# Where a decayed key product, a gate weight, a gather and a weight conversion stand in a fused linear-attention and MoE kernel

## The chip, the cores and the metric

The kernel runs on one core of a Trainium2 chip. The metric is the device time in microseconds (us) of one execution. In the text PE is TensorE, DVE is VectorE, ACT is ScalarE, GpSimd is the engine that the profile calls POOL, and SP is SyncE, which issues most of the DMAs. Each engine runs its own instructions in its own order and waits for the others through semaphores.

## What is computed

A linear attention with a decay for every channel, whose output is the input of a mixture of eight experts with one expert for each token, followed by a dense MLP with a squared relu:

```python
state = alpha[:, :, t, :, None] * state + np.einsum('bhd,bhe->bhde', k[:, :, t], v[:, :, t])
y[:, :, t] = np.einsum('bhd,bhde->bhe', q[:, :, t], state)
...
logits = x @ w_gate + modality_bias[modality_id]
e_idx = np.argmax(logits, axis=1)
...
gate_w = probs[np.arange(N), e_idx]
h = np.maximum(x[mask] @ w1[e], 0.0)
out[mask] = gate_w[mask, None] * (h @ w2[e])
...
h = x @ w_in
r = np.maximum(h, 0.0)
return (r * r @ w_out).astype(np.float32)
```

There are 4 sequences of 768 tokens with 8 heads of 48 channels, so 3072 tokens of 384 values. An expert has a hidden width of 1024, the last MLP one of 2048.

## The kernel before

**Attention.** The 3072 tokens are 24 chunks of 128, six to a sequence. `prep(n)` makes, on DVE, the running product of the decay (`acum`, a scan, L455), its reciprocal (L457), a scan in the other direction (`rs`, L459, the decay from a token to the chunk's end), the scaled queries `qt` (L461) and the scaled keys `kt` (L463). `kt` has three buffers, `rs` one. A chunk is prepared three chunks ahead of its use. `qk_mm` multiplies keys and queries on PE (`sp`, L476), ACT copies the result out (`pa`, L479), and GpSimd cuts away the future tokens (`pm`, L481, two instructions for a chunk). `k_T` transposes `kt` on PE. `kv_mm` makes the chunk's addition to the state on PE (`kv`, L502 and L506), and DVE scales the state (`sd`, L509). ACT copies it into block form (`sbd`, L516 and L517), and `y_mm` (L526, L531) makes the output `y`, which ACT copies (`yt`, L533).

**Gating.** It follows the chunks in groups of 8, 8, 5 and 3. For a group: the logits on PE (`lg`), the one-hot choice on DVE (`gate_a`, into `oh_all`), the exponentials on ACT (`gate_e`, `ex`), matmuls on PE that count each token's rank within its expert (`gate_b`, `rk`), arithmetic of seven DVE instructions on that rank (`gate_c`, L249 to L258), and the gate's weight (`gate_s`, L270 to L273: a sum, an addition and a reciprocal, `gw`). `scale(t)` then transposes a chunk's output on PE (`xtr`, L281), and two ACT instructions scale it by `gw` (`xb`, L285); SP stores it. PE writes `xtr` into a PSUM buffer that `xb` has to have read before the next `xtr`.

**Experts.** The tokens of the experts go through eight slots. Slots 0 and 1 hold 2 blocks of 128 tokens, slots 2 to 6 hold 4, slot 7 is small. `gather(i)` has GpSimd issue one indirect DMA for each block (L607), into `xg`, which has one buffer. `x_T1` transposes the gathered tokens on PE (`xt`, L625). `s1` and `s2` are the two layers, each product made of three matmuls (L632 to L634) on a high and a low half of the operands. Weights are loaded as `raw` and split into halves by ACT (L542) and DVE (L543, `w1l`, `w2l`); `pop()` does one waiting split or load.

**Conversion.** Beside the slots, the last MLP's weights, which arrive as 64-bit numbers, are converted to fp32 in 24 steps. A step is a load (`conv_load`), five DVE instructions (L694 to L698) and one ACT instruction (`conv_v`), two GpSimd products of 128x512 (`conv_g`, L705 and L706) and a store (`conv_store`). `conv_tick((2, 0, 1))` stores one block, loads another and computes a third. The tile `cvt` in which a step ends has two buffers, and the same two hold `r`, the hidden layer of the last MLP.

**The last MLP** works on six chunks of 512 tokens with 16 steps `f` each: `m1` (relu on ACT, L984; square on DVE, L985; a split) and `m2`, into `acc`. Indirect DMAs write the rows out.

**What sets the order.** It is written out by hand. The attention loop has named places in each chunk, "pre", "kv", "pool", "mid" and "end", and `at(n, place, fn)` puts work into them; `do(n, place)` runs what is there. In the loop, `qk_mm(n + 1)` comes ahead of `prep(n + 3)`, that ahead of "mid", then `y_mm(n)` and "end". In the slots the order is that of the loop over `f`, with `conv_tick` at the listed values of `f`.

Of the kernel before, what the change touches and what calls it, by code (L numbers as in the profile page):

```python
# [18 lines left out]
ALU = mybir.AluOpType  # L19
# [37 lines left out]
def body(ctx, tc, qka, v, alpha, mod, wg, mbias, w1, w2, w_in, w_out, out):  # L57
    nc = tc.nc
    V, A, G, PE, SY = nc.vector, nc.scalar, nc.gpsimd, nc.tensor, nc.sync
# [174 lines left out]
    def gate_b(g):  # L234
        t0, T = GROUPS[g]
        ohb = oh_all[:, t0:t0 + T + 1, :]
        rk = ps_g.tile([128, GM + 1, NE], F32, tag="rk", name="rk")[:, :T + 1, :]
        PE.matmul(rk, lt_b, ohb, start=True, stop=False)
        for i in range(T):
            PE.matmul(rk[:, i + 1:, :], ones_b, ohb[:, i:i + 1, :].to_broadcast([128, T - i, NE]), start=False, stop=(i == T - 1))  # L240
        gst[g]["rk"] = rk

    def gate_c(g):
        t0, T = GROUPS[g]
        sh = [128, T, NE]
        rk = gst[g]["rk"]
        oh = oh_all[:, t0:t0 + T, :]
        R = gt.tile(sh, F32, tag="R", name="R")
        V.tensor_tensor(R, rk[:, :T, :], over(run, sh), op=ALU.add)  # L249
        V.tensor_add(run, run, rk[:, T, :])  # L250
        V.tensor_mul(R, R, oh)
        ri = rk_all[:, t0:t0 + T, :]
        V.tensor_reduce(ri, R, axis=AX.X, op=ALU.max)
        V.tensor_scalar(rhx_all[:, t0:t0 + T, :], ri, 7, 3, op0=ALU.logical_shift_right, op1=ALU.bitwise_xor)
        lo = gt.tile([128, T, 1], I32, tag="lo", name="lo")
        V.tensor_single_scalar(lo, ri, 127, op=ALU.bitwise_and)
        lof = gt.tile([128, T, 1], F32, tag="lof", name="lof")
        V.tensor_copy(lof, lo)  # L258
        gst[g]["lof"] = lof
# [6 lines left out]
    def gate_s(g):  # L266
        t0, T = GROUPS[g]
        ex = gst[g]["ex"]
        ss = gt.tile([128, T], F32, tag="ss", name="ss")
        V.tensor_reduce(ss, ex, axis=AX.X, op=ALU.add)  # L270
        V.tensor_scalar_add(ss, ss, 1e-9)
        gw = gt.tile([128, T], F32, tag="gw", name="gw")
        V.reciprocal(gw, ss)  # L273
        gst[g]["gw"] = gw
# [175 lines left out]
    def prep(n):  # L450
        qk = loaded.pop(n)
        qq, kk = (qk[:, i * NP * C:(i + 1) * NP * C].rearrange("p (a c) -> p a c", c=C) for i in range(2))
        al = qk[:, 2 * NP * C:]
        acum = at2.tile([RP, NP, CA], F32, tag="acum", name="acum", bufs=3)
        V.tensor_tensor_scan(acum.rearrange("p a c -> p (a c)"), al, one0.rearrange("p a c -> p (a c)"), 0.0, op0=ALU.mult, op1=ALU.max)  # L455
        rz = raz[n % NR]
        V.reciprocal(rz[:, :, C + 1], acum[:, :, C])  # L457
        rs = at2.tile([RP, NP, CA], F32, tag="rs", name="rs", bufs=1)
        V.tensor_tensor_scan(rs.rearrange("p a c -> p (a c)")[:, ::-1], al[:, ::-1], rz.rearrange("p a c -> p (a c)")[:, ::-1], 0.0, op0=ALU.mult, op1=ALU.add)  # L459
        qt = xp.tile([RP, NP, C], F32, tag="xl", name="qt", bufs=4)  # L460
        V.tensor_mul(qt, qq, acum[:, :, 1:C + 1])  # L461
        kt = at2.tile([RP, NP, C], F32, tag="kt", name="kt", bufs=3)
        V.tensor_tensor(kt, kk, rs[:, :, 2:], op=ALU.mult)  # L463
        ae = acum[:, :, C:C + 1]
        return dict(ae=ae, qt=qt, kt=kt)

# [265 lines left out]
    def at(n, where, f):  # L732
        todo.setdefault((n, where), []).append(f)
# [16 lines left out]
    for n in range(N):  # L750
        if n + 4 < N:
            loaded[n + 4] = load(n + 4)
        if n + 3 < N:
            vs[n + 3] = load_v(n + 3)
        do(n, "pre")
        kv_mm(n)
        do(n, "kv")
        ts()
        if n + 1 < N:
            qk_mm(n + 1)  # L760
            k_T(n + 1)
        do(n, "pool")
        ts()
        if n + 3 < N:
            preps[n + 3] = prep(n + 3)
        do(n, "mid")
        if n > GROUPS[EG + 1][0] + 3:
            pop(2)
        if n == N - 1:
            x_T(0, 0)  # L770
            x_T(0, 1)
        y_mm(n)
        if n + 1 < N:
            s_bd(n + 1)
        ts()
        if n > 0:
            g, i = tile_group[n - 1]
            t0, T = GROUPS[g]
            if i % 4 == 3 or i == T - 1:
                at(n + 1, "kv", gate_lg(g, i // 4 * 4, i + 1))  # L780
            if i == T - 1:
                late = g > EG
                at(n + 1, "kv", lambda g=g: (gate_a(g), gate_e(g)))
                at(n + 1, "mid" if late else "end", lambda g=g: gate_b(g))
                at(n + 1 if late else n + 2, "end" if late else "kv", lambda g=g: (gate_c(g), gate_s(g)))
                if g == EG:
                    at(n + 2, "mid", early_plan)
                    at(n + 3, "pre", lambda: push(wload(0)))
                    at(n + 4, "mid", lambda: early.append(first_ids(EARLY, 2, ids_e)))
                    at(n + 5, "pool", lambda: (early.pop()(), gather(0)))  # L790
                d = GM if g == EG else 3 if late else 2
                for k in range(T):
                    at(n + (1 if late else 2) + k // 3, "end", lambda t=t0 + k: gate_bt(t))
                    at(n + 2 + k // d, "pre" if late else "pool", lambda t=t0 + k: todo_ts.append(t))
        do(n, "end")
# [95 lines left out]
    mm2(1, 2)  # L891
    x_T1(2, 2)
    mm2_out(1, offset(1), 2, 1)
    conv_tick((2, 0, 1))
    pop()

    soff, sac, shh = {}, {}, {}
# [27 lines left out]
    for i in range(2, NSLOT):  # L925
        last = i == NSLOT - 1
        for f in range(8):
            if f == 0:
                if i > 2:
                    s2(i - 1, 6)  # L930
                drain(("w1", i - 1))
                soff[i] = offset(i)
                perm(i, soff[i])
                if last:
                    push(load_w1(WS, lambda k: wi32[k * 128:(k + 1) * 128, 0:1024]))
                else:
                    gather(i + 1)
                    push(wload(i))
            s1(i, f)
            if f > 0:  # L940
                pop()
            if f in ((0,) if last else (2, 4, 5) if i == 2 else (0, 2, 3, 5)):
                conv_tick((2, 0, 1))
            if last and f == 2:
                push(load_w2(WS, lambda k: wo32[k * 256:(k + 1) * 256, :].rearrange("(f p) d -> p f d", p=128)))
            if f == 5:
                if last:
                    xx2[0] = xsplit(chunks[0], range(1))
                else:
                    x_T1(i + 1, 0)  # L950
            if f == 7:
                if last:
                    xx2[0] = xsplit(chunks[0], range(1, KD), xx2[0])
                else:
                    x_T1(i + 1, 1)
            if f == 1 and i > 2:
                s2(i - 1, 7)
            if f >= 2:
                s2(i, f - 2)
            if f == 7 and not last:  # L960
                x_T1(i + 1, 2)
# [80 lines left out]
    for s in range(len(steps) + LAG):  # L1042
        if s < len(steps):
            ci, f = steps[s]
            if ci > 0:
                i, j = divmod(s - 16, 4)
                if i < NALPHA:
                    if j == 0:
                        alr[i] = alpha_load(i)
                    if j > 1:  # L1050
                        alpha_range(i, j - 2, alr[i])
                elif i == NALPHA and j == 0:
                    fl = rare_flag()
                elif i == NALPHA and j == 2:
                    rare_sum(fl)
            if ci == 0:
                if f in (0, 2, 4):
                    conv_tick((2, 0, 1))
                pop()
                if f == 4:  # L1060
                    w2b()
                if f == 7:
                    drain(("w1", WS + 1))
            more = ci + 1 < len(chunks)
            if f == 13 and more:
                xx2[ci + 1] = xsplit(chunks[ci + 1], range(1))
            m1(s)
        if s >= LAG:
            ci, f = steps[s - LAG]
            if ci == 0 and f == 0:  # L1070
                drain(("w2", WS))
            if ci == 0 and f == 8:
                drain(("w2", WS + 1))
            if s - LAG < len(steps) - TAIL:
                m2(s - LAG)
# [182 lines left out]
```

## Time and profile before

| | us |
| --- | --- |
| time, median of 3 runs | 805.73 (804.85 to 806.98) |
| the profiled execution: its own time | 804.95 |
| the profiled execution: its span | 803.1 |
| PE busy in it | 764.7 |
| DVE busy | 487.1 |
| ACT busy | 336.6 |
| GpSimd busy | 185.4 |

The span runs from the first to the last instruction of the profiled execution, and the busy times are shares of it. An average over the whole kernel says little here: up to about 140 us there is attention, with DVE nearly always busy; from about 150 to 390 us there are the slots, where PE is nearly always busy and GpSimd converts; from about 394 us on there is the last MLP, almost nothing but PE. So each stage is read by itself.

### The profile page before, as it was taken

The numbers are of one execution on the slowest core, as the hardware profiler recorded it, in microseconds if no ns is written. First come the engines' busy times: TensorE is split into PE (matmuls) and PEld (weight loads), VectorE is DVE, ScalarE is ACT, GpSimd is POOL, SyncE is SP. The second block draws the span as 40 slices with busy tenths as digits, with TensorE's granted clock in tenths as the row PEclk, the third lists the DMA queues.
The fourth block names the chain that finished last, engine by engine and source line by source line (L and its number), as shares of the span: only waits on it lengthen the run. The fifth ranks groups of instructions, "written<-read, shape, count | busy, mean of one in ns | idle before, by whom it ended". The sixth has DMA issues, their size and how long they took to land.

```text
span 803.1 us, 12832 instructions
## 1 busy us (share of the span) xinstructions
PE 764.7 (95%) x5007; PEld 672.5 (84%) x5007; DVE 487.1 (61%) x811; ACT 336.6 (42%) x622; POOL 185.4 (23%) x177
## 2 busy tenths in 40 slices
PE   6998988799899999999899999999999999999995
PEld 5787867799688888889789999999999999999985
DVE  7999998468589678697773444544544343343340
ACT  2556667425344534445553332332243233333240
POOL 6344434023464444342110010010000002002001
PEclk8999999899999999999999999999999999999998
DMA  8775876157777588778530030022000001000001
GB/s 220 186 212 153 231 192 218 58 143 218 232 162 272 201 164 262 157 231 185 145 120 0 1 118 27 1 82 63 1 11 31 0 1 40 1 1 30 11 1 43
DMA packets 42557, 88.78 MB, mean 111 GB/s; under 512 B 11149, under 2 KB 26535, under 8 KB 42487
## 3 DMA queue, kind: packets, MB, share of 16 engines
q1 hardware_dynamic: 39287, 78.04, 35.1%
q0 software_dynamic: 3200, 9.83, 3.7%
q8 instruction: 41, 0.67, 0.4%
q14 instruction: 29, 0.24, 0.1%
HBM read 72.10 MB, written 15.76 MB: 109 GB/s over the span
## 4 chain that ended last, share of the span: by engine, by line
PE 75%; DVE 3%; DMA 3%; ACT 2%; issue 2%; POOL 0%; SPq 0%; POOLq 0%; ACTq 0%; DVEq 0%
PE acc L634 8%; PE acc L632 8%; PE acc L633 8%; PE h L633 8%; PE h L634 8%; PE h L632 8%; PE oo L632 4%; PE hps L632 4%; PE oo L634 4%; PE oo L633 4%; PE hps L633 4%; PE hps L634 4%; DMA xg<-xs,ids 1%; PE xt L625 1%; DMA wo<-cvt 1%
## 5 line engine op out<-in xcount | busy, mean ns | idle before, releaser
L985 DVE TENSOR_TENSOR r<-r 128x512 f32<-128x512 f32 x96 | 67.7, 705 | 147.4 <-ACT r L984 147.3
L632 PE MATMUL acc<-w2h,hh 128*128 128x384 f32 x372 | 125.4, 337 | 3.0 <-ACT hh L542 3.0
L634 PE MATMUL acc<-w2h,hl 128*128 128x384 f32 x372 | 125.7, 338 | 0.3 <-DVE hl L543 0.2
L633 PE MATMUL acc<-w2l,hh 128*128 128x384 f32 x372 | 124.9, 336 | 0.0
L984 ACT ACTIVATE r<-h 128x512 f32<-128x512 f32 x96 | 57.4, 598 | 159.5 <-PE h L634 153.9
L634 PE MATMUL h<-xh,w1l 128*128 128x512 f32 x288 | 113.8, 395 | 0.0
L633 PE MATMUL h<-xl,w1h 128*128 128x512 f32 x288 | 113.6, 395 | 0.0
L632 PE MATMUL h<-xh,w1h 128*128 128x512 f32 x288 | 112.1, 389 | 0.0
L1008 POOL DMA_INDIRECT out_dram<-ob,pidx x24 | 23.9, 997 | 366.2 <-ACT ob L1006 326.8
L543 DVE TENSOR_TENSOR hl<-r,hh 128x512 fp32r<-128x512 f32 x93 | 64.5, 694 | 63.8 <-PE acc L634 37.1
L542 ACT CAST hh<-r 128x512 fp32r<-128x512 f32 x93 | 57.7, 620 | 78.7 <-DVE r L985 78.7
L632 PEld LDWEIGHTS acc<-w2h,hh 128*128 128x128 f32 x372 | 69.9, 188 | 7.8 <-ACT hh L542 3.8
L633 PEld LDWEIGHTS acc<-w2l,hh 128*128 128x128 f32 x372 | 69.8, 188 | 3.8
L634 PEld LDWEIGHTS acc<-w2h,hl 128*128 128x128 f32 x372 | 69.8, 188 | 0.9 <-DVE hl L543 0.9
L632 PE MATMUL oo<-hh,w2h 128*128 128x512 f32 (+1 forms) x192 | 69.3, 361 | 0.0
L632 PE MATMUL hps<-xh,w1h 128*128 128x512 f32 (+1 forms) x192 | 68.0, 354 | 1.2 <-ACT xb L285 0.7
L481 POOL TENSOR_SCALAR_AFFINE_SELECT pm<-pa 128x512 f32<-128x512 f32 x48 | 52.1, 1108 | 73.0 <-ACT pa L479 72.9
L634 PE MATMUL oo<-hh,w2l 128*128 128x512 f32 (+1 forms) x192 | 67.7, 353 | 0.0
L633 PE MATMUL oo<-hl,w2h 128*128 128x512 f32 (+1 forms) x192 | 67.6, 352 | 0.0
L633 PE MATMUL hps<-xl,w1h 128*128 128x512 f32 (+1 forms) x192 | 67.1, 350 | 0.0
L634 PE MATMUL hps<-xh,w1l 128*128 128x512 f32 (+1 forms) x192 | 67.1, 349 | 0.0
L634 PEld LDWEIGHTS h<-xh,w1l 128*128 128x128 f32 x288 | 54.0, 187 | 11.5
(220 smaller groups left out, 1360.2 us busy)
## 6 DMA issues: line engine op xcount, KB each, us to landing
qk<-qka_dram SPq DMA_DIRECT2D x23, 675.5 KB, 5.3
raw<-w_dram SPq DMA_DIRECT2D x21, 512.0 KB, 5.7
raw<-w_dram SPq DMA_DIRECT2D x28, 384.0 KB, 3.5
cvr<-w_in_dram SPq DMA_DIRECT2D x12, 512.0 KB, 7.0
cvr<-w_out_dram SPq DMA_DIRECT2D x12, 512.0 KB, 11.1
vv<-v_dram SPq DMA_DIRECT2D x24, 192.0 KB, 6.3
xs<-xb SPq DMA_DIRECT2D x24, 192.0 KB, 3.1
alr<-alpha_dram SPq DMA_DIRECT2D x9, 512.0 KB, 3.7
```

The lines of the kernel that those rows point to most:

```text
L481: G.affine_select(out=pmt, in_=pa, pattern=[[0, 4], [1, C]], compare_op=ALU.is_ge, fill=0.0, base=0, channel_multiplier=-1)
L542: A.copy(hi, raw)
L543: V.tensor_sub(lo, raw, hi)
L625: PE.transpose(xt[:, hf * 128:(hf + 1) * 128], xgs[i][:, hf, k * 128:(k + 1) * 128], ident)
L632: PE.matmul(o, ah, bh, start=start, stop=False)
L633: PE.matmul(o, ah, bl, start=False, stop=False)
L634: PE.matmul(o, al, bh, start=False, stop=stop)
L984: A.activation(r, o, AF.Relu)
L985: V.tensor_mul(r, r, r)
L1008: G.indirect_dma_start(out=out, out_offset=bass.IndirectOffsetOnAxis(ap=pidx[:, n:n + 1], axis=0), in_=ob, in_offset=None)
```

## The change

It has four parts.

1. The product `kt` (L463) is made by GpSimd, not by DVE. The operands and the buffers are the same.
2. The gate's weight `gate_s` moves. For the first two groups it stood with `gate_c` in the "kv" place two chunks on; now it stands at the "end" of the chunk before, right behind the rank matmuls. For the last two groups it moves from "end" to "mid" of the same chunk.
3. The conversion's steps move: the one ahead of slot 2 is gone, slot 2 has four (it had three), slots 3 to 6 have five each (they had four), slot 7 and the last MLP's first chunk have none (they had one and three). All 24 are done by slot 6.
4. The second half of the `w_out` load of the last MLP (`w2b`) is put in the list at step 1 of the first chunk, not at step 4.

```diff
@@ prep
         kt = at2.tile([RP, NP, C], F32, tag="kt", name="kt", bufs=3)
-        V.tensor_tensor(kt, kk, rs[:, :, 2:], op=ALU.mult)
+        G.tensor_tensor(kt, kk, rs[:, :, 2:], op=ALU.mult)
@@ attention loop
-                at(n + 1, "mid" if late else "end", lambda g=g: gate_b(g))
-                at(n + 1 if late else n + 2, "end" if late else "kv", lambda g=g: (gate_c(g), gate_s(g)))
+                at(n + 1, "mid" if late else "end", lambda g=g: (gate_b(g), gate_s(g)))
+                at(n + 1 if late else n + 2, "end" if late else "kv", lambda g=g: gate_c(g))
@@ ahead of slot 2
     mm2_out(1, offset(1), 2, 1)
-    conv_tick((2, 0, 1))
     pop()
@@ slots
-            if f in ((0,) if last else (2, 4, 5) if i == 2 else (0, 2, 3, 5)):
+            if not last and f in ((2, 3, 4, 5) if i == 2 else (0, 2, 3, 5, 6)):
                 conv_tick((2, 0, 1))
@@ last MLP
             if ci == 0:
-                if f in (0, 2, 4):
-                    conv_tick((2, 0, 1))
                 pop()
-                if f == 4:
+                if f == 1:
                     w2b()
```

GpSimd's queue at the start of the attention stage, as a difference. The first row kept belongs to the gate's constants, `kt` is the key product and `pm` the mask:

```order
 L180 MEMSET run 128x8
 L181 MEMSET oh_all 128x200
-L481 AFFINE_SELECT pm<-pa 128x512 x44
+L463 TENSOR_TENSOR kt<-qk,rs 112x512
+L481 AFFINE_SELECT pm<-pa 128x512 x2
+L463 TENSOR_TENSOR kt<-qk,rs 112x512
+L481 AFFINE_SELECT pm<-pa 128x512 x2
+L463 TENSOR_TENSOR kt<-qk,rs 112x512
+L481 AFFINE_SELECT pm<-pa 128x512 x2
```

A key product now stands ahead of each pair of masks, and the third of them stands behind the block of constants.

DVE's queue where the first group's weight `gw` is made, before. `R` to `lof` are the rank arithmetic, `sd` is the state:

```order
L461 TENSOR_TENSOR qt<-qk,acum 112x512
L463 TENSOR_TENSOR kt<-qk,rs 112x512
L509 TENSOR_TENSOR sd<-kv,acum 112x192
L249 TENSOR_TENSOR R<-rk,run 128x64
L250 TENSOR_TENSOR run<-run,rk 128x8
L251 TENSOR_TENSOR R<-R,oh_all 128x64
L253 TENSOR_REDUCE rk_all<-R 128x8
L254 TENSOR_SCALAR rhx_all<-rk_all 128x8
L256 TENSOR_SCALAR lo<-rk_all 128x8
L258 CAST lof<-lo 128x8
L270 TENSOR_REDUCE ss<-ex 128x8
L271 TENSOR_SCALAR ss<-ss 128x8
```

The same place after:

```order
L461 TENSOR_TENSOR qt<-qk,acum 112x512
L270 TENSOR_REDUCE ss<-ex 128x8
L271 TENSOR_SCALAR ss<-ss 128x8
L273 RECIPROCAL gw<-ss 128x8
L509 TENSOR_TENSOR sd<-kv,acum 112x192
L249 TENSOR_TENSOR R<-rk,run 128x64
L250 TENSOR_TENSOR run<-run,rk 128x8
```

The weight's three instructions went ahead of `sd` and of the seven rank instructions, and `kt` left this queue.

GpSimd's queue from the end of the attention stage to slot 2, before. The two rows of `ids_b` are the gather of slot 1, the next four that of slot 2, the last four that of slot 3; `cvr` and `cvt` are the conversion:

```order
L607 DMA xg<-xs,ids_b 128x384 x2
L607 DMA xg<-xs,ids 128x384 x4
L705 TENSOR_TENSOR cvr<-cvr,cvt 128x512
L706 TENSOR_TENSOR cvt<-cvr 128x512
L705 TENSOR_TENSOR cvr<-cvr,cvt 128x512
L706 TENSOR_TENSOR cvt<-cvr 128x512
L607 DMA xg<-xs,ids 128x384 x4
```

The same place after:

```order
L607 DMA xg<-xs,ids_b 128x384 x2
L607 DMA xg<-xs,ids 128x384 x4
L705 TENSOR_TENSOR cvr<-cvr,cvt 128x512
L706 TENSOR_TENSOR cvt<-cvr 128x512
L607 DMA xg<-xs,ids 128x384 x4
L705 TENSOR_TENSOR cvr<-cvr,cvt 128x512
L706 TENSOR_TENSOR cvt<-cvr 128x512
```

The gather of slot 3 stands behind one step of the conversion and no longer behind two.

## Rows read from the trace of the kernel before

**Rows 1.** The page's busy times: engine, busy us, share of the span, instructions.

```profile
PE 764.7 (95%) x5007; PEld 672.5 (84%) x5007; DVE 487.1 (61%) x811; ACT 336.6 (42%) x622; POOL 185.4 (23%) x177
```

**Rows 2.** PE's waits: waiting instruction, what ended the wait, us in total, times, longest.

```profile
PE xtr L281 <- ACT xb L285: 9.2, 6, 3.6
...
PE xt L625 <- DMA xg<-xs,ids: 3.0, 4, 1.4
PE acc L632 <- ACT hh L542: 3.0, 2, 2.3
```

**Rows 3.** Windows: stretch, length, busy of PE, PEld, DVE, ACT, POOL, granted clock, DMA.

```profile
20.00:67.00 47.00, 45.44 (x652) 38.20 (x647) 45.75 (x70) 25.83 (x57) 21.64 (x21) 1.00 0.71 190
...
70.30:73.80 3.50, 3.50 (x26) 3.28 (x27) 3.50 (x7) 2.58 (x7) 1.01 (x2) 0.51 0.55 156
...
142.00:148.90 6.90, 5.76 (x34) 5.24 (x34) 3.38 (x10) 2.95 (x7) 0.00 (x0) 0.51 0.15 57
...
217.10:220.60 3.50, 3.04 (x9) 2.36 (x9) 1.48 (x4) 0.68 (x2) 0.00 (x0) 0.51 1.05 392
220.60:360.00 139.40, 139.40 (x638) 115.33 (x637) 111.91 (x160) 64.29 (x103) 66.56 (x48) 1.00 0.75 206
```

**Rows 4.** GpSimd's timeline at the start: start us, us, engine, line, instruction.

```profile
17.94 0.26 POOL L181 MEMSET oh_all<- 128x200 bf16 x1
```

**Rows 5.** Groups by line and shape: count, busy us, mean ns, idle before.

```profile
L481 POOL TENSOR_SCALAR_AFFINE_SELECT pm<-pa 128x512 f32<-128x512 f32 x48 | 52.1, 1108 | 73.0 <-ACT pa L479 72.9
...
L455 DVE TENSOR_TENSOR_SCAN acum<-qk,one 112x520 f32<-112x520 f32 x24 | 31.6, 1318 | 6.4 <-DMA qk<-qka_dram 6.0
L459 DVE TENSOR_TENSOR_SCAN rs<-qk,raz 112x520 f32<-112x520 f32 x24 | 30.6, 1273 | 0.8
...
L461 DVE TENSOR_TENSOR qt<-qk,acum 112x512 f32<-112x512 f32 x24 | 19.1, 794 | 0.0
...
L463 DVE TENSOR_TENSOR kt<-qk,rs 112x512 f32<-112x512 f32 x24 | 18.2, 758 | 0.0
```

**Rows 6.** GpSimd's timeline: a mask pair at 109, conversion products at 201 and 209.

```profile
109.26 1.23 POOL L481 TENSOR_SCALAR_AFFINE_SELECT pm<-pa 128x512 f32<-128x512 f32 x2 [1.39 <-ACT pa L479]
...
201.32 1.70 POOL L706 TENSOR_TENSOR cvt<-cvr 128x512 f32<-128x512 f32 x1
...
209.93 1.04 POOL L706 TENSOR_TENSOR cvt<-cvr 128x512 f32<-128x512 f32 x1
```

**Rows 7.** PE's timeline: the same matmuls in two chunks that follow each other.

```profile
47.90 1.16 PE L476 MATMUL sp<-qt,kt 48*128 48x128 f32 x16
...
52.63 1.16 PE L476 MATMUL sp<-qt,kt 48*128 48x128 f32 x16
```

**Rows 8.** DVE's timeline at the first group's rank arithmetic and weight.

```profile
66.88 0.21 DVE L249 TENSOR_TENSOR R<-rk,run 128x64 f32<-128x64 f32 x1
...
68.51 0.20 DVE L273 RECIPROCAL gw<-ss 128x8 f32<-128x8 f32 x1
```

**Rows 9.** ACT's timeline at the first group and the late group; brackets: idle before.

```profile
68.81 0.73 ACT L285 ACTIVATE xb<-xtr,gw 128x192 f32<-128x192 f32 x2 [3.08 <-DVE gw L273]
...
139.87 0.35 ACT L517 COPY sbd<-sd 48x192 f32<-48x192 f32 x1
142.36 0.73 ACT L285 ACTIVATE xb<-xtr,gw 128x192 f32<-128x192 f32 x2 [2.14 <-issue]
```

**Rows 10.** PE's timeline at the transposes of the first two groups.

```profile
69.60 0.60 PE L281 MATMUL xtr<-ident,yt 112*128 112x112 f32 x4 [2.59 <-ACT xb L285]
...
112.22 0.60 PE L281 MATMUL xtr<-ident,yt 112*128 112x112 f32 x4 [1.76 <-ACT xb L285]
```

**Rows 11.** The chain of work that ended last, at slot 2.

```profile
207.56 10.06 DMA xg<-xs,ids
```

**Rows 12.** Groups by line and shape: the longest DVE instruction of a conversion step.

```profile
L697 DVE SCALAR_TENSOR_TENSOR cvr<-cvr,cvt 128x512 int32<-128x512 int32 x24 | 16.6, 694 | 0.8
```

**Rows 13.** ACT's timeline at the start of the last MLP.

```profile
393.95 0.60 ACT L984 ACTIVATE r<-h 128x512 f32<-128x512 f32 x1 [4.58 <-DMA wo<-cvt]
```

## Prediction

> **What bounds the kernel now.** I read the page's busy times first: TensorE (PE) is busy 764.7 of 803.1 us [rows 1]. Of a kernel bound in this way, only two things can be won without changing its matmuls: stretches in which PE waits, and stretches in which its clock is at the lower level. The list of PE's waits gives the first: 9.2 us before `xtr`, the transposes of the gating stage, which wait until ScalarE (ACT) has scaled the tile before (`xb`); 3.0 before `xt`, which waits for gathered tokens; 3.0 before `acc`, which waits for ACT in the final MLP [rows 2]. The table of windows gives the second. [...] The same table says how close the others are: VectorE (DVE) is busy 45.75 of 47 us in the attention stage (20 to 67) and PE 45.44, so there DVE has hardly any room; in the MoE slots DVE is busy 111.91 of 139.40 beside a PE without a gap [rows 3].
>
> **The change part by part.**
>
> *Startup.* The product `kt` of the third chunk now stands in GpSimd's queue behind the gate's constants, whose last operation ends at 18.2 [rows 4], and ahead of the masks (`pm`) of the chunk before. The mask of that chunk, and with it its `y`, comes later by one product: between 0 if PE has other work, and 1.70, the longer of the two prices below. I take a third, +0.6.
>
> *kt on GpSimd.* DVE loses 24 products of 0.758, 18.2 us [rows 5]; none of that is PE's time, as long as PE is not waiting. GpSimd gains 24 products. The nearest rows for their price are the conversion's products on GpSimd, also two fp32 inputs of 512 columns: 1.04 at 209.93, with DVE idle, and 1.70 at 201.32, with DVE's `w2l` and `hl` beside it [rows 6]. The mask pair takes 2 x 1.108 on average [rows 5] and 1.23 undisturbed [rows 6]. GpSimd's work for a chunk is then 2.2 + 1.04 to 1.70 = 3.3 to 3.9 us, and a chunk lasts 52.63 - 47.90 = 4.73 [rows 7], so GpSimd has room. DVE's four products and scans take 1.318 + 1.273 + 0.794 + 0.758 = 4.14 [rows 5] and fall to 3.39, less whatever the meeting with GpSimd's product gives back. A new wait comes in: there is one buffer `rs`, so the next chunk's `rs` scan on DVE waits until GpSimd has read the last one. Behind it in DVE's queue stand `qt` and `sd`, for which PE waits. Between two `rs` scans DVE has `qt`, `sd` and `acum`, over 2 us, against a product of 1.04 to 1.70; only when a mask pair stands ahead of the product does the wait show. The product itself is made more than a chunk ahead of the matmuls `sp` that read it, so a late product delays PE through `sd` first. I take +1.5 for the 23 chunks, with 0 and +5 (0.2 a chunk) as ends.
>
> [...]
>
> *The gate weight ahead of the rank arithmetic, groups 0 and 1.* In the first group `gw` starts at 68.51, behind the rank arithmetic that began at 66.88 [rows 8], and `xb` waits for it 3.08 and starts at 68.81 [rows 9]; PE then waits 2.59 for `xtr`, and 1.76 in the second group [rows 10]. In the new order `sd` (0.35) and the seven rank operations (66.88 to 68.06) stand behind `gw`, and `kt` (0.76) is not on DVE at all. That is 0.35 + 1.2 + 0.76 = 2.3 us earlier for `gw`; in the first group 0.3 of the wait could stay, in the second none. What was behind, `sd`, becomes 0.6 later against the rank's order but not against before, since `kt` has left. The gain is 2.59 + 1.76 = 4.35; at least half of it if ACT's own queue comes in the way (-2.2), at most -5.5 if the small waits beside them go too (`xtr` waits 9.2 in total, 3.63 of it in the late group). Behind the first wait PE is at 0.51 for 3.50 us, all of it busy [rows 3]; at full clock that work takes half, so -1.75. The second wait, 1.76 long, is followed by no such stretch.
>
> *The late group.* `xb` starts at 142.36 after an idle time of 2.14, though ACT was done with `sbd` at 139.87 + 0.35 = 140.22 [rows 9], and its `xtr` waits 3.63, the longest of the six waits on ACT [rows 2]. The weight now comes ahead of two `w2l` splits and the rank arithmetic, so `xb` can start when ACT is free: -2.1, -1.0 if the tokens' gather or `sd` is late next. About 1.5 of the wait stays. The stretch of 6.90 behind it at 0.51 holds 5.76 of busy PE [rows 3]; without the drop it takes half, -2.9, and 0 if the stretch stays. I take the first, since no such stretch follows the 1.76 of the second group [rows 10].
>
> *The gather ahead of the conversion.* Before, GpSimd works on a conversion product at 201.32 [rows 6] ahead of the gather of slot 3, whose last part is issued at 207.56 and lands 10.06 later [rows 11], and PE waits 3.0 for it in four steps [rows 2]. With one conversion (GpSimd's two products, 1.0 to 1.7 each [rows 6], and their wait for DVE) taken out of the way, the issue comes over 3 us earlier, so the 3.0 go: -3.0, or -2.0 if the transfer meets other loads. The clock stretch behind it holds 3.04 of busy PE at 0.51 [rows 3]: -1.5, or 0.
>
> *The conversion in slots 2 to 6.* They had 19 steps of the 24 and have 24. One more step in a slot costs DVE five operations of at most 0.69 each, 3.5 at most [rows 12], and GpSimd two. In the four slots or so of 220.6 to 360 DVE is busy 111.91 of 139.40 [rows 3]; with four more steps it is 125.9 at most, 90%. The rest of DVE's idle time there covers it. +1.0, with 0 and +5 (1 us in each slot) as ends.
>
> *The final MLP.* In its first chunk ACT's first `r` waits 4.58 for the store of a converted block, since both use the tile `cvt` [rows 13], and PE waits 3.0 for `acc` [rows 2]. With no conversion left there, both go: -3.0 (-2.3 if only the longest wait goes, -3.2 with the small one behind it). The second half's `w2` is loaded earlier; its splits are not needed before the ninth step, so 0.
>
> **The sum**, against the profiled execution (804.95; its span is 803.1, the rest lies around it): +0.6 + 1.5 - 4.35 - 1.75 - 2.1 - 2.9 - 3.0 - 1.5 + 1.0 - 3.0 = -15.5. The median of the runs is 805.73, 0.8 above the profiled one; I put the same difference on it: 805.7 - 15.5 = 790.2. All ends on the good side together give -5.5 - 1.75 - 2.1 - 2.9 - 3.0 - 1.5 - 3.2 = -20, so 785.8; all on the bad side +1.7 + 5 - 2.2 - 1.0 - 2.0 + 5 - 2.3 = +4.2 (no clock stretch gone), so 810.
>
> **The rivals.**
>
> *A. DVE and GpSimd exclude each other in the attention stage.* If no such pair overlapped, a chunk would take acum, rs and qt, 3.39, plus a mask pair of 1.23 plus a product of 1.04: 5.66 in place of 4.73. For it: masks stretch from 1.23 to 2.2 beside DVE [rows 5, 6]. Against it: by the same account the old chunk would need 4.14 + 1.23 = 5.37, and it took 4.73, paced by PE [rows 7]. In full it costs 23 x 0.93 = 21 us, and a third of the 6.1 us won at the first two groups goes with it; startup and the new wait's +1.5 are inside it: 790.2 + 21 + 2 - 1.5 = 812. It makes the kernel slower than before once a chunk grows by more than 0.76 us. Range of this case 807 to 815.
>
> *B. The extra conversion steps make the slots late.* If DVE's 3.5 for each of the five added steps showed whole, +17.5 in place of +1.0; if half, +8.7, so 798. For it: DVE is busy four fifths of the slots. Against it: PE has no gap in 220.6 to 360 [rows 3], where four steps a slot already run.
>
> *C. The attention waits only change their releaser.* `xtr` then waits for `sd`, ACT or the product, and the clock stretches at 70.3 and 142 stay. Of the terms above, only the gather and the final MLP keep their gain, with half of the late group's first term: 805.7 - 3.0 - 1.5 - 3.0 - 1.0 + 3.1 = 800, between 796 and 803.
>
> **How the numbers follow.** Forecast as reckoned, 785 to 796: 0.58. C: 0.18. B: 0.10, 794 to 803. A: 0.12. In 2 of the remaining 100, something else. The predicted time is 790.2. A range from 785 to 803 takes in the forecast, B and C and leaves out A, so it holds about 0.85. A difference of 0.3%, 2.4 us, is what a measurement of this kernel can tell from none; so faster is under 803.3, slower over 808.1. The forecast, C and B but for their upper ends give faster 0.81; same 0.08; slower 0.11, nearly all of A.
>
> **What would show it.** Right: no `xtr` wait over 1 us in the two early groups; the granted clock 1.00 in what were the stretches at 70.3, 142 and 217.1; no `xt` wait for `xg` of slot 3, and no `acc` wait at the start of the final MLP; chunks of 4.73 still, with DVE well under 97% busy in the attention stage. Wrong: chunks of 5 us and more, with `rs` waiting for GpSimd or `sp` for `kt` (A); gaps of PE in the slots behind `w1l`, `w2l` or `hl` (B); `xtr` waits of the old length under other names (C).

## The result: slower by 1.1%

The changed kernel takes 815.87 us in the median of 4 runs (815.17 to 816.40); the kernel before takes 806.36 beside it (804.85 to 807.74). The ratio is 1.0108, with a 95% interval of 1.0075 to 1.0141. The forecast was 790.2, in a range from 785 to 803. The profiled execution of the changed kernel took 816.4, its span is 814.7 us.

The page's busy times, as in [rows 1]:

```profile
PE 768.5 (94%) x5007; PEld 674.3 (83%) x5007; DVE 494.9 (61%) x787; ACT 337.7 (41%) x622; POOL 217.5 (27%) x201
```

DVE lost 24 instructions (811 to 787) and is busy 7.8 us longer (487.1 to 494.9). The product left DVE and its time did not. PE's idle time rose from 38.4 to 46.2, the span less the busy time, and PE's busy time by 3.8 though its instructions are the same; 2.7 of these are clock, by the windows below.

PE's waits, as in [rows 2] (waiting instruction, what ended the wait, us in total, times, longest):

```profile
PE kv L502 <- DVE sd L509: 5.1, 4, 2.1
PE hps L633 <- DVE xl L543: 3.8, 2, 2.2
PE xt L625 <- DVE xl L543: 3.7, 1, 3.7
PE xtr L281 <- ACT xb L285: 3.7, 5, 1.5
PE sp L476 <- POOL kt L463: 3.4, 3, 1.8
PE lg L214 <- ACT ls L209: 3.3, 4, 1.4
```

The wait for `xb` did fall, from 9.2 to 3.7, and the wait for `acc` is gone. In their place stand waits for DVE, for the state `sd` and for `xl`, and one for `kt`, which is now GpSimd's.

The windows around the stretches at the lower clock, as in [rows 3] (length, busy of PE, PEld, DVE, ACT, POOL, granted clock, DMA):

```profile
36.90:43.90 7.00, 6.96 (x54) 5.93 (x55) 6.73 (x9) 1.77 (x4) 3.75 (x3) 0.51 0.55 146
...
135.90:142.90 7.00, 4.94 (x34) 4.08 (x32) 4.72 (x7) 3.13 (x6) 2.25 (x3) 0.51 0.67 194
...
234.90:241.90 7.00, 5.77 (x16) 4.71 (x17) 5.70 (x9) 0.59 (x1) 5.45 (x5) 0.51 1.02 129
```

The stretches at 70, 142 and 217 are gone and three others have come, at 37, 136 and 235, each at a new wait: the first begins where the wait ends, the other two while PE still waits. In the first of them a chunk's `sp` takes 2.08 us (at 38.86), ahead of it 1.16 (at 31.22). The three hold 17.7 us of busy PE where the old ones held 12.3; at half speed, an estimate from the granted 0.51, that is 2.7 us more.

Where the new waits begin, DVE's timeline shows (start us, us, engine, line, instruction):

```profile
27.00 2.80 DVE L461 TENSOR_TENSOR qt<-qk,acum 112x512 f32<-112x512 f32 x1
29.72 0.34 DVE L509 TENSOR_TENSOR sd<-kv,acum 112x192 f32<-112x192 f32 x1
...
33.45 1.20 DVE L186 CAST modf<-mod_sb 128x24 f32<-128x24 int32 x1
```

and GpSimd's beside it:

```profile
24.36 3.15 POOL L481 TENSOR_SCALAR_AFFINE_SELECT pm<-pa 128x512 f32<-128x512 f32 x2
27.48 1.18 POOL L463 TENSOR_TENSOR kt<-qk,rs 112x512 f32<-112x512 f32 x1
28.62 1.67 POOL L481 TENSOR_SCALAR_AFFINE_SELECT pm<-pa 128x512 f32<-128x512 f32 x2
```

`qt`, which the by-form mean of before puts at 0.794 [rows 5], takes 2.80 while GpSimd has masks, product and masks without a break; `sd` behind it starts at 29.72. The cast of 128x24 numbers at 33.45, beside the next product, takes 1.20; in the trace before it took 0.17. PE's timeline shows what that does:

```profile
30.12 0.58 PE L502 MATMUL kv<-sd,ident 112*112 112x192 f32 x2 [1.14 <-DVE sd L509]
...
36.94 0.97 PE L502 MATMUL kv<-sd,ident 112*112 112x192 f32 x2 [2.13 <-DVE sd L509]
```

Two waits of 1.14 and 2.13, and a stretch at 0.51 that begins at the end of the second and costs half of its 6.96: 6.8 us together; at its seventh chunk the kernel is 6.4 us behind the one before (`sp` at 46.4 against 40.0).

Not all of that is the change's. Four of the kernels below (e5, e9, e13, e15) have the attention code of before, and in their profiles, too, PE waits 1.8 us for `sd` at this place and a stretch at the lower clock begins at 35 or 36. In e9's, whose seventh `sp` starts at 42.4:

```profile
34.48 0.58 PE L502 MATMUL kv<-sd,ident 112*112 112x192 f32 x2 [1.81 <-DVE sd L509]
```

So a single pair of profiles does not price this place; the repeated runs below do that for the part as a whole.

### The profile page after: what moved, and what is told of

Read it like the earlier page. It is cut to its first block, busy times and chain, and to the rows that moved or that the text cites. A ratio compares the mean times of both kernels' runs of the same rounds, so it can differ in the third digit from the quotient of the medians.

```text
span 814.7 us, 12893 instructions
## 1 busy us (share of the span) xinstructions
PE 768.5 (94%) x5007; PEld 674.3 (83%) x5007; DVE 494.9 (61%) x787; ACT 337.7 (41%) x622; POOL 217.5 (27%) x201
## 4 chain that ended last, share of the span: by engine, by line
PE 75%; DVE 10%; DMA 7%; issue 2%; ACT 2%; POOL 0%; SPq 0%; POOLq 0%; DVEq 0%; ACTq 0%
PE h L633 8%; PE h L634 8%; PE acc L634 8%; PE acc L632 8%; PE acc L633 8%; PE h L632 8%; PE hps L633 3%; PE hps L632 3%; PE hps L634 3%; PE oo L633 3%; PE oo L634 3%; PE oo L632 3%; PE sp L476 2%; PE y L531 2%; PE y L526 2%
## 5 line engine op out<-in xcount | busy, mean ns | idle before, releaser
L543 DVE TENSOR_TENSOR hl<-r,hh 128x512 fp32r<-128x512 f32 x93 | 64.4, 692 | 63.9 <-PE acc L634 38.4
L633 PEld LDWEIGHTS h<-xl,w1h 128*128 128x128 f32 x288 | 54.0, 188 | 9.2
```

Source lines behind the costliest of these rows:

```text
L543: V.tensor_sub(lo, raw, hi)
L633: PE.matmul(o, ah, bl, start=False, stop=False)
```

## Experiments

A ratio below is that of a kernel to the kernel before on the same chip, with its 95% interval; 0.1% is 0.8 us. Each kernel has a short name, given in brackets where it first stands.

### One part at a time

The key product alone (e1). The edit is the diff's first part:

```diff
-        V.tensor_tensor(kt, kk, rs[:, :, 2:], op=ALU.mult)
+        G.tensor_tensor(kt, kk, rs[:, :, 2:], op=ALU.mult)
```

> The kernel before with one edit: the key product on GpSimd. Theory T (in the trace after, DVE instructions that meet a key product of GpSimd are stretched, bt_all from 0.85 to 2.6 us, qt once to 2.8, and the state sd comes late): 811 to 819 us, with DVE's attention work hardly shorter. Rival U (the key product is harmless, the loss lies in the conversion steps alone): 803 to 808. Rival V (the gate weight ahead of sd is what makes the state late): 803 to 808 too.

Measured: 1.0107 (1.0048 to 1.0166), 814.94 us. This line by itself loses as much as the whole change.

The gate weight alone, the diff's second part (e2), and the same kernel again in more rounds (e17):

> The kernel before with one edit: the gate weight gate_s right behind the rank matmuls. Theory T and rival U: the transposes' waits of 2.59, 1.76 and 3.63 shrink and the clock stretches behind the first and the last go, 796 to 801 us. Rival V (the weight's three instructions ahead of sd cost more than they give): 806 or more.

> e2's kernel again (the gate weight alone), in more rounds: 0.995 to 0.998 of before, an interval below 1.

Measured: 0.9971 (0.9938 to 1.0004), then 0.9968 (0.9951 to 0.9984). It is a gain, of 0.3%, which is 2.6 us; theory and rival U had expected 4.7 or more. The waits of PE in e2:

```profile
PE xtr L281 <- ACT xb L285: 4.7, 6, 1.5
...
PE lg L214 <- ACT ls L209: 2.5, 2, 1.8
```

The waits for `xb` lose 4.5 us. But in this profile ACT comes to its later `xb` sooner and stands for the store that has to free the buffer, in ACT's timeline:

```profile
125.47 0.73 ACT L285 ACTIVATE xb<-xtr,gw 128x192 f32<-128x192 f32 x2 [1.10 <-DMA xs<-xb]
126.09 0.27 ACT L209 COPY ls<-lt 128x128 f32<-128x128 f32 x1
```

Behind it waits `ls`, and PE waits 1.76 for that, where it waited 0.7 before. In e2's profile the clock stretch that stood at 142 stands at 127, with the same length, and the one at 70 has not gone.

The profile of e17, the same kernel, reads otherwise. The wait for `xb` is 4.2 there, ACT does not wait for the store, and the longest wait for `ls` is 0.7, as before. The clock does not fall at 70 or 127, but does at 82, 134 and 219 (columns as in the windows above):

```profile
66.00:75.00 9.00, 7.68 (x101) 6.55 (x101) 8.72 (x22) 6.37 (x16) 4.08 (x4) 1.00 0.40 129
82.00:89.00 7.00, 6.59 (x41) 5.92 (x43) 6.86 (x11) 2.60 (x7) 3.09 (x2) 0.54 0.62 183
...
134.00:141.00 7.00, 6.68 (x42) 5.23 (x44) 2.71 (x5) 1.84 (x5) 1.78 (x3) 0.53 0.65 175
219.00:226.00 7.00, 4.85 (x12) 3.33 (x13) 3.67 (x6) 3.05 (x6) 0.00 (x0) 0.51 1.05 392
```

So the shorter `xb` waits are found twice, and the chain over the store and `ls` only once. Why the gain is 2.6 us and not more stays open.

The conversion alone, the diff's third and fourth parts (e3):

> The kernel before with the conversion's edits alone (gather of slot 3 ahead of one more step, five steps a slot, none in slot 7 and the last MLP, the last w_out load earlier). Theory T (steps at neighbouring f wait for the store of the block two before, since cvt has two buffers; DVE stands still, its queue comes late and PE waits): 809 to 814 us. Rival U (the whole loss is here): 814 to 818. By the prediction on record, without the attention's part: 799 to 801.

Measured: 1.0033 (1.0001 to 1.0066). The forecast's sum for these parts was below 1.

The changed kernel with the key product back on DVE (e4):

> The changed kernel with the key product back on DVE. Theory T: 802 to 807 us, as e2's gain and e3's loss nearly cancel. Rival U: 808 to 812. Rival V: 814 to 818, as the changed kernel.

Measured: 0.9974 (0.9942 to 1.0005), 804.45 us. Within their intervals the parts add: +1.07 - 0.3 + 0.33 is 1.10%, and the change measures 1.08; e2 and e3 together would give +0.03, and e4 has -0.26.

The profiles tell in which stage each part acts. The slots begin with the first transpose of gathered tokens (`xt`), the last MLP with its first product `h`:

| profile | first `xt` at, us | from there to the first `h` | from the first `h` to the last |
| --- | --- | --- | --- |
| before | 143.9 | 243.5 | 390.7 |
| changed | 151.1 | 251.5 | 386.4 |
| key product (e1) | 154.1 | 241.4 | 390.3 |
| gate weight (e2, e17) | 143.1, 148.4 | 239.4, 244.1 | 390.9, 391.6 |
| conversion (e3) | 143.7 | 249.1 | 386.4 |
| gate weight and conversion (e4) | 146.1 | 248.6 | 386.4 |

A difference has to be held against what profiles with the same code in a stage differ by. The nine profiles with the attention code of before have their first `xt` between 143.7 and 147.2; e1's is at least 6.9 later. The seven with the old number of steps in each slot, the products on GpSimd and steps in the last MLP take 239.4 to 245.5 us from there to the first `h`; the five with five steps in slots 3 to 6 and the products on GpSimd take 248.6 to 257.6. And the last MLP takes 390.3 to 391.6 with steps in it, 386.4 to 387.1 without, 4.3 us less from before to changed: this term of the change is a gain. The loss lies in the attention stage and in the slots. The gate weight's 2.6 us is smaller than what single profiles differ by, and only the many runs show it.

### Why a product on GpSimd costs so much

An idle product on GpSimd beside DVE's own (e8):

```diff
         V.tensor_tensor(kt, kk, rs[:, :, 2:], op=ALU.mult)
+        du = at2.tile([RP, NP - 1, C], F32, tag="du", name="du", bufs=1)
+        G.tensor_tensor(du, kk[:, :NP - 1], qq[:, :NP - 1], op=ALU.mult)
```

> The kernel before, with its own key product on DVE, and an idle product of three quarters of the size on GpSimd in every chunk, into a tile that nobody reads; it adds work and changes no result. Theory T (GpSimd's product holds up DVE's instructions, whoever needs it): DVE's instructions in the attention stage are stretched as in e1, 812 to 822 us. Rival D (what costs is that the key product comes late, or that rs has one buffer): nobody waits here, 803 to 808.

Measured: 1.0238 (1.0189 to 1.0288), 826.46 us, above theory T's own range. Nobody waits for this product, and it has no share in `rs`. By groups of line and shape, e8 shows DVE's own key product:

```profile
L463 DVE TENSOR_TENSOR kt<-qk,rs 112x512 f32<-112x512 f32 x24 | 29.7, 1239 | 0.0
```

It was 758 ns before [rows 5]. DVE has the same 811 instructions as before and is busy 20.0 us longer, 507.1 against 487.1 [rows 1]:

```profile
PE 774.2 (94%) x5007; PEld 679.6 (83%) x5007; DVE 507.1 (62%) x811; ACT 336.6 (41%) x622; POOL 217.3 (26%) x201
```

So GpSimd's work beside DVE is enough to cost time, though nobody waits for its result. Which instructions it meets depends on where it falls: `bt_all`, stretched in e1, is not stretched here (354 ns). A late product may add to it in e1, where PE waits 3.3 us for `kt` against 1.5 before; no run parts the two there.

The key product in two halves (e7):

```diff
-        V.tensor_tensor(kt, kk, rs[:, :, 2:], op=ALU.mult)
+        for h in range(2):
+            G.tensor_tensor(kt[:, 2 * h:2 * h + 2], kk[:, 2 * h:2 * h + 2], rs[:, 2 * h:2 * h + 2, 2:], op=ALU.mult)
```

> e1's kernel (the key product on GpSimd, nothing else) with that product in two instructions of 112x256 each. If a DVE instruction that meets GpSimd's product is held up until that one instruction ends, and can go on between two, its stretch halves: bt_all 1.7 in place of 2.6 us, 808 to 812 us. If DVE stays held up as long as GpSimd has another instruction ready, or the cost lies in the product's lateness: 813 to 817, as e1.

Measured: 1.0078 (1.0044 to 1.0113), 814.77 us. This lies between the two, and its interval overlaps e1's; the first three `bt_all` took 2.2 us here, against 2.6 in the changed kernel and 3.0 in e1. It does not tell whether DVE can go on between two instructions of GpSimd.

### Why the conversion lost

First the theory that steps at neighbouring `f` wait for the store that frees `cvt`. Slot 2's steps were spread (e5):

```diff
-            if not last and f in ((2, 3, 4, 5) if i == 2 else (0, 2, 3, 5, 6)):
+            if not last and f in ((0, 2, 4, 5) if i == 2 else (0, 2, 3, 5, 6)):
```

> e3's kernel (the conversion's edits alone) with slot 2's four steps at f 0, 2, 4, 5 in place of 2, 3, 4, 5; nothing else. Theory T (a step right behind another waits for the store of the block two before, whose DMA is slow while the gather runs; DVE stands still and xt waits for xl): DVE's wait of 4.75 us and PE's of 3.5 in slot 2 go, with the clock stretch behind them, 801 to 804 us. Rival W (any fourth step in slot 2 is too much work for DVE): the wait stays, 806 to 808.

Measured: 1.0058 (1.0024 to 1.0093). In slot 2 it did what the theory says: PE's wait there fell from 3.5 to 1.6 and the clock stretch behind it went. But the total is no better than e3's, since PE waits where slots 3 to 6 begin, as its list of waits says:

```profile
PE hps L633 <- DVE xl L543: 6.6, 4, 3.6
```

The gather alone, the old number of steps in slots 3 to 7 and in the last MLP (e9):

```diff
-    conv_tick((2, 0, 1))
     pop()
...
-            if f in ((0,) if last else (2, 4, 5) if i == 2 else (0, 2, 3, 5)):
+            if f in ((0,) if last else (0, 2, 4, 5) if i == 2 else (0, 2, 3, 5)):
```

> The kernel before with the conversion step that stood ahead of slot 2 moved behind slot 2's first layer-one block, so that the gather of slot 3 stands ahead of it in GpSimd's queue; the later steps stay where they were. By the prediction on record its third part alone: the 3.0 us of waits for xg and the clock stretch behind them go, 801 to 803. Rival X (the earlier gather meets the conversion's loads and the slot's weights on the DMA queues and delays them): 805 to 808.

Measured: 0.9994 (0.9969 to 1.0019), nothing. The gather's wait shrinks, and another of DVE's comes, in PE's timeline at slot 2:

```profile
218.24 0.33 PE L625 MATMUL xt<-ident,xg 128*128 128x128 f32 x1 [0.49 <-DMA xg<-xs,ids]
219.26 0.33 PE L625 MATMUL xt<-ident,xg 128*128 128x128 f32 x1 [0.69 <-DMA xg<-xs,ids]
231.93 0.66 PE L625 MATMUL xt<-ident,xg 128*128 128x128 f32 x4 [1.60 <-DVE xl L543]
235.89 0.50 PE L633 MATMUL hps<-xl,w1h 128*128 128x512 f32 x1 [0.31 <-DVE xl L543]
```

The sum of these is 3.1, against 3.0 before. The 3.0 is itself one profile's: with the gather in its old place the wait for `xg` is 1.6 in e1, 2.2 in e2 and 4.7 in e17.

The fifth step of a slot at `f` 1 instead of 6, in e5's kernel (e13):

```diff
-            if not last and f in ((0, 2, 4, 5) if i == 2 else (0, 2, 3, 5, 6)):
+            if not last and f in ((0, 2, 4, 5) if i == 2 else (0, 1, 2, 3, 5)):
```

> e5's kernel with the fifth conversion step of slots 3 to 6 at f 1 in place of f 6. If the place is what costs (two steps at f 5 and 6 lie ahead of xl, which PE needs at the next slot's start): PE's waits for xl at the ends of these slots go, 0.997 to 1.000 of before (e5 had 1.0058). If the amount is what costs (five steps a slot): 1.003 to 1.007.

Measured: 1.0095 (1.0057 to 1.0133). The waits moved from `xl` to `hl` (11.4 us) and grew. The amount costs, not the place.

The same kernel with GpSimd's products left out (e15):

```diff
-        G.tensor_tensor(lf, lf, f, op=ALU.mult)
-        G.tensor_tensor(f, lf, hf, op=ALU.add)
```

> e13's kernel (five steps a slot, the fifth at f 1; 1.0095 of before) with GpSimd's two products left out of each step, so that the last weights are wrong; loads, DVE's five instructions, ACT's one and the stores stay. If what makes the slots late is DVE held up by GpSimd's products: PE's waits for hl and xl in the slots go, 0.995 to 1.000. If it is DVE's own five instructions or their wait for the stores: 1.005 or more.

Measured: 0.9882 (0.9851 to 0.9913), 17 us below e13 by the two ratios; only these two instructions of a step differ. In e13 DVE is busy 495.6 us with 811 instructions, in e15 470.9 with as many. DVE's groups in e13:

```profile
L543 DVE TENSOR_TENSOR w1l<-raw,w1h 128x1024 fp32r<-128x1024 f32 x27 | 41.9, 1555 | 7.6 <-ACT w1h L542 7.6
...
L694 DVE TENSOR_SCALAR cvt<-cvr 128x512 int32<-128x512 int32 x24 | 17.6, 733 | 29.2 <-issue 11.6 <-DMA wi<-cvt 10.5 <-DMA wo<-cvt 5.3
```

and in e15:

```profile
L543 DVE TENSOR_TENSOR w1l<-raw,w1h 128x1024 fp32r<-128x1024 f32 x27 | 32.8, 1219 | 4.7 <-ACT w1h L542 4.7
...
L694 DVE TENSOR_SCALAR cvt<-cvr 128x512 int32<-128x512 int32 x24 | 10.2, 424 | 35.3 <-DMA wi<-cvt 21.7 <-DMA wo<-cvt 11.2 <-DMA cvr<-w_in_dram 2.3
```

Without the products the `w1l` splits take 1219 in place of 1555 ns and the steps' first instruction 424 in place of 733. And the wait of that first instruction for the stores has grown, from 15.8 to 32.9 us, while PE's waits in the slots for `hl` and `xl` have fallen from 15.5 to 2.6. So the stores, on which the theory rested, are not what makes the slots late; DVE had time to wait for them. That theory falls, and so does DVE's own work as the whole cause, for its five instructions are still there. GpSimd's products take its place, as in the attention stage.

### Where else the steps could go

In slot 7, in place of the last MLP (e10); with the gate weight (e11); and with the gather first as well (e12):

```diff
-            if f in ((0,) if last else (2, 4, 5) if i == 2 else (0, 2, 3, 5)):
+            if f in ((0, 2, 4, 6) if last else (2, 4, 5) if i == 2 else (0, 2, 3, 5)):
...
-                if f in (0, 2, 4):
-                    conv_tick((2, 0, 1))
```

> The kernel before with the three conversion steps of the last MLP's first chunk moved into slot 7 (at f 2, 4, 6 beside the one at 0). If the wait for acc (2.1 to 2.4 us, and 0.6 at the next square) is due to those steps and slot 7 has room for them: both go, 0.996 to 0.997 of before. If slot 7 has no room, its own waits of PE take their place: 0.999 to 1.003.

> e10 with the gate weight right behind the rank matmuls as well. If the two gains add: 0.993 to 0.995 of before (e2 alone gave 0.997). If the freed time is taken back by another wait: 0.997.

> e11 with the gather of slot 3 ahead of one more conversion step (slot 2's steps at f 0, 2, 4, 5 and none ahead of it). e9, that edit alone, gave 0.9994 of before, since a wait of xt for DVE's xl came in the place of the one for the gather: so as e11, within 0.001. If the later steps in slot 7 leave DVE free there: 0.002 better than e11.

Measured: 1.0055 (1.0024 to 1.0086), 1.0006 (0.9971 to 1.0042) and 0.9996 (0.9968 to 1.0024). Slot 7 has no room: in e10 PE waits there for `hl`, three times in all,

```profile
PE oo L633 <- DVE hl L908: 6.5, 3, 2.6
```

with a clock stretch at 396 behind it. The last MLP does get shorter, 387.1 us from its first `h` to its last, but that is not enough.

The last MLP without any conversion step, bought by leaving two steps out (e14):

```diff
+            if last and f == 2:
+                i0 = cvn[2]
+                for q in range(i0, 24):
+                    SY.dma_start((wi32, wo32)[q // 12].rearrange("a b -> (a b)").rearrange("(o p f) -> o p f", p=128, f=TB)[q % 12], cvr[i0])
...
-                if f in (0, 2, 4):
-                    conv_tick((2, 0, 1))
```

> e9's kernel (gather of slot 3 first) with the last two of the 24 conversion steps left out, so that none stands in the last MLP; their blocks are written with another block's values. It gives the price of the conversion in the last MLP by itself. By the prediction's sixth part (the waits for acc, 3.0 us): 0.996 to 0.997 of before. If another wait takes their place: 0.999 to 1.000.

Measured: 0.9913 (0.9887 to 0.9940); e9, the same but for this, had 0.9994. So the last MLP does give something when the steps are gone from it and stand nowhere else: between 3.5 and 9.5 us by the two intervals; the profiles in the table above put it at 4.3, against 3.0 in the forecast. They have to stand somewhere, though, and wherever they were put they cost as much or more.

### The products on DVE

If GpSimd's products cost DVE more than they are worth, DVE should make them itself. The kernel before with one edit (e18), then with the gate weight (e19), then the changed kernel with all products on DVE (e20):

```diff
-        G.tensor_tensor(lf, lf, f, op=ALU.mult)
-        G.tensor_tensor(f, lf, hf, op=ALU.add)
+        V.tensor_tensor(lf, lf, f, op=ALU.mult)
+        V.tensor_tensor(f, lf, hf, op=ALU.add)
```

> The kernel before with the conversion's two products made by DVE instead of GpSimd, nothing else. DVE gets two instructions of about 0.7 us a step, and loses what GpSimd's products cost it: w1l 2.01 to 1.22, the first instruction of a step 1.26 to 0.42. If that is an even trade, 0.995 to 1.002 of before; if DVE's own longer queue is what decides in the slots, 1.003 or more.

> e18 with the gate weight right behind the rank matmuls (e17 gave 0.997 by itself): the product of the two ratios, 0.992 to 0.999.

> The changed kernel with both kinds of products on DVE: the key product back there, and the conversion's two products moved there; the gate weight's move, the gather first and five steps a slot stay. If GpSimd's products are what made the five steps a slot late (e15 left them out: 0.988), the slots have room, the last MLP is free of steps, and the forecast's gains outside the attention products show: 0.985 to 0.993 of before. If DVE's seven instructions a step are too many: 1.000 or more.

Measured: 0.9941 (0.9912 to 0.9970), 0.9938 (0.9910 to 0.9966) and 1.0073 (1.0042 to 1.0105). Taking work from GpSimd and giving it to the engine that is four fifths busy in the slots (111.91 of 139.40 us [rows 3]) makes the kernel faster, by 0.6%. In e18 DVE got 48 instructions of 0.69 us, 33.3 us in all, and its busy time rose by 14.9 only, from 487.1 to 502.0; the other 18.4 it got back from its own instructions. e18's and e19's lists of PE's waits hold nothing in the slots but 2.2 and 2.0 us of `xt` for `xl`, and waits below 1 us. With five steps a slot it is too much again: in e20 PE waits for `xl` where slots begin,

```profile
PE hps L633 <- DVE xl L543: 6.7, 3, 2.9
```

so both the engine and the amount matter. e19 is the best of the kernels here; it beats the kernel before by 0.3 to 0.9% and, by the two ratios, the changed one by 1.7%. It is not measurably better than e18, so the gate weight's 0.3% does not show on top of it.

## The prediction, step by step

**The step that failed first is "kt on GpSimd", +1.5 with 0 and +5 as ends.** Alone it measured +1.07%, 8.6 us. The prediction summed what GpSimd has to do in a chunk, found room, and wrote that DVE falls to 3.39 us "less whatever the meeting with GpSimd's product gives back". That last quantity was left at that, and it was the one that decided. The by-form rows of the changed kernel, to be held against [rows 5]:

```profile
L455 DVE TENSOR_TENSOR_SCAN acum<-qk,one 112x520 f32<-112x520 f32 x24 | 37.7, 1569 | 5.9 <-DMA qk<-qka_dram 5.5
L463 POOL TENSOR_TENSOR kt<-qk,rs 112x512 f32<-112x512 f32 x24 | 37.1, 1546 | 34.8 <-DVE rs L459 34.8
...
L459 DVE TENSOR_TENSOR_SCAN rs<-qk,raz 112x520 f32<-112x520 f32 x24 | 30.3, 1264 | 4.2 <-POOL kt L463 1.9
...
L461 DVE TENSOR_TENSOR qt<-qk,acum 112x512 f32<-112x512 f32 x24 | 22.1, 919 | 0.0
...
L293 DVE TENSOR_SCALAR bt_all<-rev,lof,tokid 128x128 f16<-128x128 f32 x24 | 14.2, 641 | 0.1
```

and `bt_all` in the kernel before:

```profile
L293 DVE TENSOR_SCALAR bt_all<-rev,lof,tokid 128x128 f16<-128x128 f32 x24 | 7.6, 369 | 0.0
```

`acum` costs 6.1 more, `qt` 3.0, `bt_all` 6.6: 15.7 of the 18.2 us that the product took on DVE are given back by three other groups, and the casts and small products beside a meeting give back more. In e1, with this part alone, DVE is busy 492.6 us, 5.5 more than before with 24 instructions less. The product's price on GpSimd was right (1.546, between the 1.04 and 1.70 taken), and so was the wait that the +1.5 was for, that of `rs` for GpSimd, 1.9 us on DVE. The stretch of DVE's other instructions had no term. The old trace had rows for it, `kt` on DVE with masks of GpSimd beside it and without:

```profile
50.09 1.12 DVE L463 TENSOR_TENSOR kt<-qk,rs 112x512 f32<-112x512 f32 x1
...
59.48 0.69 DVE L463 TENSOR_TENSOR kt<-qk,rs 112x512 f32<-112x512 f32 x1
```

The bound of +5 was drawn over all chunks alike. The steady ones kept their pace: the matmuls of [rows 7] follow each other by 58.70 - 54.07 = 4.63 in the changed kernel. In e1's profile 14 of the 23 distances between the chunks' `sp` lie within 0.2 us of before's, and seven are longer by 0.8 to 2.9, most of them where DVE has something more to do (the bias at 33, the second group's gating and the early plan at 108 to 131). Profiles with the old attention code differ from each other in the same two places, so how the 8.6 us divide among the chunks is not shown.

**Rival A** had the right engines, the right sign and a range (807 to 815) that the time just exceeds, but the wrong place: it put the cost into every chunk, 5.66 in place of 4.73, and the steady chunks did not grow. It was given 0.12. The row that spoke against it, the old chunk's 4.73 beside an exclusive account of 5.37, was weaker than it looked, since the 4.14 in that account is a sum of means that hold the stretch by the masks already (`kt` 0.69 and 1.12 above); it was read as if the meeting cost little. The rival's account held only `acum`, `rs` and `qt` beside GpSimd's work, while the cast and `bt_all` were stretched too, 0.17 to 1.20 us and 369 to 641 ns.

**The conversion, +1.0 with 0 and +5 as ends,** failed for the same reason. The prediction counted DVE's five instructions, 3.5 at most, against DVE's idle time of 220 to 360. It left out what GpSimd's two products do to DVE's other instructions in that time, though the row of 1.70 against 1.04 [rows 6] had been read, from GpSimd's side alone. e3 came out at +0.33%, 2.7 us, with the last MLP's gain of 4.3 in it and nothing from the gather (e9), so the five added steps cost about 7 us, an estimate from these numbers. Rival B had this mechanism half right: the slots are late, but e15 has DVE's five instructions and no such loss. Its range, 794 to 803, left out its own full case, 790.2 + 16.5 = 806.7.

**The gather, -3.0 and -1.5:** the wait for `xg` shrank, and the wait for `xl` took its place in the same slot, which no rival had named (B spoke of the added steps). e9: nothing.

**The gate weight, -4.35 - 1.75 - 2.1 - 2.9 = -11.1:** 0.3% measured, 2.6 us. Of the 6.45 us of waits booked, the waits for `xb` lost 4.5 in e2 and 5.0 in e17: the late group's 3.63 fell to 1.5, as worked out, the first group's 2.59 to 1.3 only. The term that failed outright is the clock: -4.65 was booked for stretches that would go, and in e2's profile one stays and one stands elsewhere, while in e17's both are gone and two others stand in the attention stage, at 82 and 134. What brings a stretch where it comes stays open. Rival C had said that the waits change their releaser, and for `lg` in e2 they do.

**Right were** the final MLP's term (the wait for `acc` goes, and the stage is 4.3 us shorter against the -3.0 forecast) and the sign of the early groups' waits, the longest of which is 1.2 in the changed kernel, a little over the 1 us named. Startup's +0.6 is not settled: `sp` of the third chunk starts at 20.8 against 20.1 before, but e3, with the old attention code, has it at 19.1.

The misses add up. Against the forecast, the key product with startup is worse by 8.6 - 2.1 = 6.5 us, the added steps by 6, the gather by 4.5, the gate weight by 8.5, and the last MLP better by 1.3: 24 in all, where the forecast of -15.5 and the measured +9.5 lie 25 apart.

## What to carry to other kernels

Before work is moved from DVE to GpSimd to unload DVE, look in the trace for what DVE's instructions take with and without GpSimd at work, and charge the difference to every DVE instruction that the moved work will meet; here a GpSimd instruction of 1.5 us cost DVE all of the 0.76 us that its move had saved. An engine's idle share does not say that it can take work at no cost to the others: GpSimd was busy 23% of the span [rows 1], and the product it took cost 8.6 us (e1). And where DVE is nearly full, try the other direction first: here two products taken from GpSimd and given to DVE made the kernel 0.6% faster. Last, take the waits and clock stretches of one profile as one draw: two profiles of the same kernel (e2, e17) had them in different places.

## What the runs showed of the hardware

That DVE's instructions take longer beside GpSimd's fp32 product had been allowed for, in rival A above all; the size had not. A cast of 128x24 on DVE went from 0.17 to 1.20 us beside one, `qt` from 0.67 (before, at 54.20) to 2.80 between masks, product and masks in a row, and two products of 128x512 per conversion step were worth 17 us of 817 (e13 against e15). Not expected either was that DVE could stand 33 us for stores in e15 while PE waited 2.6 us for `hl` and `xl` in the slots. And the stretches at the lower granted clock, 0.51 to 0.54 in the windows above, came elsewhere: the profile before has three (at 70, 142 and 217), the changed kernel's three others (37, 136 and 235), and the two profiles of one kernel, e2 and e17, have those of the attention stage at different places (70 and 127; 82 and 134). So a gain that rests on a stretch's going is worth little until a run shows it.
